# Attention kernel: whole-array products in a row instead of alternating with products on half the columns

## The chip, the cores and the metric

The kernel runs on one core of a Trainium2 chip. The metric is the device time of one execution in microseconds (us), as a median of runs; the profile is one further look at a single execution, with its own span. Engines are named as in the profile: PE is TensorE's matmuls, PEld its weight loads, DVE VectorE, ACT ScalarE, POOL GpSimd, SP the queue that issues most DMAs.

## The reference

A linear attention with a decaying state (2 batch rows, 8 heads, 768 tokens, head width 48) feeds a layer with 4 experts of width 1024, which feeds a two-layer network of width 2048. Only the attention is touched by the change:

```
for t in range(S):
    cur = einsum('bhd,bhe->bhde', u * k[t], v[t])
    y[t] = einsum('bhd,bhde->bhe', r[t], state + cur)
    state = w * state + einsum('bhd,bhe->bhde', k[t], v[t])
x = y, rows of all heads together            # 1536 tokens x 384
x = sum over e of p[:, e] * (relu(x @ w1[e]) @ w2[e])
out = elu(x @ w_in) @ w_out
```

## The kernel before, in words

The attention goes in chunks of 128 tokens, 6 to a batch row, 12 in all (`ci` from 0 to 11; `c` is the chunk's place in its batch row). For a chunk it makes a matrix A of 128 x 128 for each head from scaled r and k (`s2`, L251; then `s2p`, L258, copies it out of the banks under a mask, on DVE, onto a diagonal that POOL has written, L233). It then needs, for a pair of heads, S^T r (the state with the past, L306) plus v^T A (the chunk's own part, L312), summed in one PSUM bank. `s3u` (L272) makes the state's change, and `s3s` (L293, L295, on DVE) the next state S from it.

In `s3` the product with S fills the array: its stationary operand is 112 rows by 112 columns, both heads of a pair at once. The products with A have 48 columns, one head in the lower and one in the upper 64 columns, side by side. For each of the 4 pairs, one product on the whole array is followed by two on halves of the columns. Products are in fp32, and the trace has two records, each with a weight load of its own, for one product. Where `c` is 0 (chunks 0 and 6) there is no past, and the S products fall away. `s3` runs for chunks 2 to 11, so 9 of them have S products: 2, 3, 4, 5, 7, 8, 9, 10, 11.

The first two chunks go another way, before the layers start (`s3f`, L353 and L354): the rows of x are made directly in three groups of 128 (`kk`), each first in products on 64 columns, side by side, then one product on the whole array, which adds the diagonal part `va`. Then `s3x` casts the result (ACT, L468) and makes its low part (DVE, L469), which is the first layer's first operand.

The order is written out by hand. The layers' products (`st1`, L610, and `st2`, L646, on the whole array) go in steps; in the first expert's blocks of 256 tokens one or two attention steps (`a1` with `s2`; `a2`; `a3` with `s3`) are placed behind a step's first product until the attention is over. Every engine runs its instructions in the order of the program, and DVE also splits the weights for the layers (`work`, L505) between the attention's steps. The banks of the attention are three, taken in turn (`bank()`).

```
for p in range(NP):
    if c:
        nc.tensor.matmul(py[0:112, p, :], S of the pair, r of the pair, start=True, stop=False)
    for j in range(2):
        nc.tensor.matmul(py[64 * j:64 * j + m, p, :], v of head 2p + j, A[:, j, p, :], ...)
```

Of the kernel before, what the change touches and what calls it, by code (L numbers as in the profile page):

```python
# [22 lines left out]
P = 128  # L23
B, H, S, D = 2, 8, 768, 48
NP = H // 2          # head pairs; a pair sits on partitions 0-47 and 64-111
NCB = S // P         # 128-token chunks of a batch row
NCH = B * NCB
N = B * S            # tokens
DM = H * D
KD = DM // P  # L30
NE, FF = 4, 1024     # experts, their width
NU = NE + 2          # the second layer's 2048 columns count as two more units
NF = FF // P
NX = 6               # slots for weights in the attention's room
WARM = 12            # products of zeros ahead of the first
NS = (2, 1, 2, 1, 1, 1, 1, 1)    # the attention's steps by step of the layers' first block
BA, BB = 1, 2        # the steps of a block that no weights are split in
TB = 512             # tokens of a block
# [8 lines left out]
# the upper words of float64s, read as float32s: of the largest and the least normal float32  # L47
# [3 lines left out]
class Fast:  # L51
    """Attention in chunks of 128 tokens, decays as w^t and w^-(s+1), which
    needs W_LO <= w <= W_HI (elsewhere w is held there, and the general path is taken).

    Rows of a pair of heads: 64 j + (index in the head). The chunk's part of a head's output,
    with its index on the rows, is v^T A + S^T r, where A[s, t] is (k_s w^-(s+1)).(r_t w^t)
    for s < t and r.u.k for s = t."""
# [27 lines left out]
    def bank(self):  # L85
        """The next bank: of three, and of the two layers' while those wait for the first x."""
        pool, tag = self.banks[self.nbank % len(self.banks)]
        self.nbank += 1
        return pool.tile([P, 512], F32, tag=tag, name=tag)

    def warm(self, n):
        """Products of zeros: the array's clock is halved while it has little to do."""
        nc = self.g.nc
        if self.zero is None:
            self.zero = self.c.tile([P, 512], BF16, name="zero")
            nc.vector.memset(self.zero, 0.0)
        pz = self.g.php.tile([P, 512], F32, tag="ph1", name="ph1")
        for _ in range(n):
            nc.tensor.matmul(pz, self.zero[:, 0:P], self.zero, start=True, stop=True)

    # r, k with their index on the rows
# [9 lines left out]
    # r, k, or v, with the tokens on the rows  # L111
# [49 lines left out]
    def setup_masks(self):  # L161
        nc = self.g.nc
        # 1 where t > s
        mf = self.c.tile([P, P], F32, name="mf")
        nc.gpsimd.memset(mf, 0.0)
        nc.gpsimd.affine_select(
            out=mf, in_=mf, compare_op=ALU.is_ge, fill=1.0, base=0,
            pattern=[[-1, P]], channel_multiplier=1)
        nc.gpsimd.tensor_copy(self.mask, mf)
# [25 lines left out]
    # r or k, scaled  # L195
# [9 lines left out]
    # the keys decayed to the chunk's end  # L205
# [6 lines left out]
    # r.u.k, by entries  # L212
# [8 lines left out]
    # the diagonal  # L221
    def s1d(self, ci):
        nc = self.g.nc
        a0 = self.p2.tile([P, H], F32, tag="a0", name="a0")
        nc.vector.tensor_reduce(out=a0, in_=self.st[ci]["uk"], axis=AX.X, op=ALU.add)  # L225
        if ci < 2:
            # the first chunks' diagonal goes by itself
            self.va[ci] = va = self.p2.tile([P, DM], F32, tag="va", name="va")
            nc.vector.tensor_tensor(
                out=va.rearrange("t (h d) -> t h d", h=H), in0=self.v[ci].rearrange("t (h d) -> t h d", h=H),  # L230
                in1=a0.rearrange("s (h o) -> s h o", o=1).to_broadcast([P, H, D]), op=ALU.mult)
            return
        nc.gpsimd.tensor_tensor(  # L233
            out=self.A[ci % 2].rearrange("s j p t -> s p j t"),
            in0=self.g.ident.rearrange("s (a b t) -> s a b t", a=1, b=1).to_broadcast([P, NP, 2, P]),
            in1=a0.rearrange("s (p j o) -> s p j o", j=2, o=1).to_broadcast([P, NP, 2, P]), op=ALU.mult)
# [6 lines left out]
    def s2(self, ci):  # L243
        nc = self.g.nc
        st = self.st[ci]
        # a bank for each of the two places of a head in its pair
        self.pa[ci] = pa = [self.bank().rearrange("q (p t) -> q p t", p=NP) for j in range(2)]
        for p, j in ([(p, j) for j in range(2) for p in range(NP)] if ci < 2 else
                     [(p, j) for p in range(NP) for j in range(2)]):
            a = 64 * j  # L250
            nc.tensor.matmul(  # L251
                pa[j][:, p, :], st["k"][a:a + D, p, :], st["r"][a:a + D, p, :], start=True, stop=True)
# [7 lines left out]
    # the state's change, and the state  # L260
    def s3u(self, ci):
# [5 lines left out]
        # side by side, a head of a pair in each half of the array's columns  # L267
# [30 lines left out]
    def s3(self, ci):  # L298
# [5 lines left out]
        for p in range(NP):  # L304
            if c:
                nc.tensor.matmul(  # L306
                    py[0:112, p, :], self.S[:, p].rearrange("q j e -> q (j e)")[:, 0:112],
                    st["r"][0:112, p, :], start=True, stop=False)
            for j in range(2):
                # at first, all rows up to the second head's are to be written  # L310
                h, m = 2 * p + j, D if c or j else 64
                nc.tensor.matmul(  # L312
                    py[64 * j:64 * j + m, p, :], v[:, h * D:h * D + m], A[:, j, p, :],
                    start=not c, stop=True)
# [5 lines left out]
        if o:  # L320
            # the rows of all heads together, by way of DRAM
# [8 lines left out]
    # the first chunks': the rows of all heads together at once, v and S between zeros  # L330
# [5 lines left out]
    def s3f(self, ci):  # L336
# [3 lines left out]
        for kk in range(KD):  # L340
            # side by side, 64 rows of x in each half of the array's columns
# [8 lines left out]
            for n in range(max(map(len, ops))):  # L350
                for i, o in enumerate(ops):
                    if n < len(o):
                        nc.tensor.matmul(px[64 * i:64 * (i + 1), kk, :], *o[n], start=not n, stop=False)  # L353
            nc.tensor.matmul(  # L354
                px[:, kk, :], self.va[ci][:, kk * P:(kk + 1) * P], g.ident, start=False, stop=True)
# [8 lines left out]
class General:  # L364
    """Attention for any w: each state entry's recurrence is scanned along the tokens, with
    the key's index on the partitions and one column of the state at a time."""
# [8 lines left out]
    def run(self, ident, xT):  # L375
# [5 lines left out]
        # sel[:, e]: from row e, 64 + e to the rows of their halves; one: from the rows of a  # L381
        # half, with the window that starts at 64 - e, to row e, 64 + e
# [69 lines left out]
class Gen:  # L452
# [40 lines left out]
    def split(self):  # L493
        """The next slice's two parts, in steps; each yields the time it takes of DVE."""
# [15 lines left out]
        # a float64 as two words: a = sign, exponent and the upper 20 fraction bits as a  # L510
        # float32 (0 below its normal range, its largest above), c = the 32 bits below
# [28 lines left out]
    def work(self, budget):  # L540
        """Splits ahead, as far as there are slots, for about so much time of DVE."""
# [25 lines left out]
    def probs(self, dp):  # L567
# [7 lines left out]
        # by expert, then tokens  # L575
# [41 lines left out]
    def evac(self, u, n, ph):  # L617
# [8 lines left out]
        else:  # L626
# [4 lines left out]
            # exp(min(h, 0)) - 1 is 0 where h > 0, and at least h elsewhere  # L631
# [57 lines left out]
    def count(self, c):  # L689
        """How many of w's entries the fast attention holds for."""  # L690
# [13 lines left out]
    def setup(self, ctx):  # L704
# [13 lines left out]
        # slices in the order of their splits: (unit, layer, slice)  # L718
# [3 lines left out]
    def setup2(self, ctx):  # L722
        """What the attention's room is for once it is over."""
# [9 lines left out]
    def layers(self, tb0, before):  # L733
        """Both layers, the first unit in blocks of tb0 tokens. before(u, t0, f) is called
        ahead of a step and gives what is to come after its first product, if anything."""
        pend = []
        for u in range(NU):
            n = TB if u else tb0
            for t0 in range(0, N, n):
                for f in range(NF):  # L740
# [3 lines left out]
                    # the end of a block frees its banks before anything else  # L744
# [15 lines left out]
    def fast(self):  # L760
        tc, nc = self.tc, self.nc
        with ExitStack() as ctx:
# [21 lines left out]
            # attention; the first two chunks before the layers start  # L784
# [30 lines left out]
            self.work(0.1)   # w1, slice 0  # L815
# [7 lines left out]
            self.work(0.1)   # w2, slice 0  # L823
# [24 lines left out]
            for i in range(2, NCH):  # L848
                steps += [(f, c) for f, c in ((a1, i), (a2, i + 1), (a3, i)) if c < NCH]
                if i % 2 == 0 and i > 2:  # L850
                    # two steps after the last a3 of a pair
# [62 lines left out]
def laid_out(r, k, v, w, u, moe_domain_probs, moe_w1, moe_w2, moe2_w_in, moe2_w_out):  # L914
    def heads(a):       # head entries to rows 64 j + d of the pairs, 0 between
# [5 lines left out]
    # by chunk: rows 64 j + d, then r or k, pair, token; and rows of tokens, then r, k, v, entry  # L921
# [11 lines left out]
    # slices of 256 hidden columns: unit, slice, layer, row, then 768 values  # L933
# [31 lines left out]
```

## Time and profile before

| | |
|---|---|
| median of 3 runs | 686.3 us (685.81 to 689.27) |
| span of the profiled execution | 685.3 us; its own time is not listed beside it, the fastest run is 685.81 |
| PE busy | 666.9 us, 3701 records |
| PEld busy | 557.4 us |
| DVE, ACT, POOL busy | 352.6, 211.5, 208.0 us |
| L306, L312 (`s3`) on PE | 16.8 and 17.7 us busy, 72 and 160 records |
| L353, L354 (`s3f`) on PE | 8.3 and 3.9 us busy, 64 and 12 records |

A record's busy time on PE is from its start to its modelled end; records overlap, so what a stretch costs is read from one start to the next. The span is cut into stages by what PE does: the first two chunks (to about 25 us), the attention among the first layer steps (about 25 to 131 us), then the layers alone.

### The profile page before, as it was taken

How to read it: one execution, taken by the hardware profiler on the slowest of the kernel's cores; microseconds unless marked ns; L12 is line 12 of the kernel's file. 1: busy time of each engine (PE TensorE's matmuls, PEld its weight loads, DVE VectorE, ACT ScalarE, POOL GpSimd, SP SyncE). 2: the span in 40 equal slices, each digit the busy share in tenths (PEclk: the TensorE clock that was granted, in tenths of full speed). 3: DMA queues.
4: the chain of work that ended last, by engine and by line, in shares of the span. 5: the costliest groups of instructions: out<-in, count | busy, mean ns of one | idle time of the engine just before them, and what ended most of it. 6: DMA issues, size and time to landing. Idle time of an engine off the chain costs nothing.

```text
span 685.3 us, 9098 instructions
## 1 busy us (share of the span) xinstructions
PE 666.9 (97%) x3701; PEld 557.4 (81%) x3701; DVE 352.6 (51%) x505; ACT 211.5 (31%) x358; POOL 208.0 (30%) x163
## 2 busy tenths in 40 slices
PE   8999999999999999999999999999997999999996
PEld 5788988899888888888888887888875888888884
DVE  7896566324544133422135696569596848212121
ACT  3232221123332113211122123133535454644441
POOL 5564563210002020202021225243744534333331
PEclk7899999999999999999999999999998999999999
DMA  8775542102421003210010221202121100001011
GB/s 256 216 215 165 171 148 69 34 15 70 162 92 47 0 3 107 99 47 0 1 55 38 93 92 47 92 7 88 46 92 46 47 0 1 0 1 47 0 47 52
DMA packets 18661, 48.11 MB, mean 70 GB/s; under 512 B 2145, under 2 KB 7698, under 8 KB 18610
## 3 DMA queue, kind: packets, MB, share of 16 engines
q1 hardware_dynamic: 18464, 47.42, 21.4%
q8 instruction: 31, 0.51, 0.3%
q14 instruction: 20, 0.16, 0.1%
q10 hardware_dynamic: 146, 0.03, 0.0%
HBM read 43.09 MB, written 4.35 MB: 69 GB/s over the span
## 4 chain that ended last, share of the span: by engine, by line
PE 84%; DVE 9%; issue 3%; POOL 2%; ACT 1%; DMA 0%; DVEq 0%; POOLq 0%; ACTq 0%
PE po L646 38%; PE ph L610 37%; PE pa L251 2%; PE pa L306 2%; PE pa L312 2%; DVE raw L519 1%; POOL acc L667 1%; DVE q L530 1%; DVE a L523 1%; DVE g L632 1%; DVE q L520 1%; DVE a L534 1%; DVE hl L623 1%; DVE a L527 1%; POOL wl L535 1%
## 5 line engine op out<-in xcount | busy, mean ns | idle before, releaser
L646 PE MATMUL po<-hh,wh 128*128 128x512 f32 (+1 forms) x504 | 183.4, 364 | 4.9 <-ACT acc L684 4.6
L646 PE MATMUL po<-hl,wh 128*128 128x512 f32 (+1 forms) x504 | 181.9, 361 | 1.9 <-POOL hl L635 1.7
L646 PE MATMUL po<-hh,wl 128*128 128x512 f32 (+1 forms) x504 | 181.5, 360 | 0.0
L610 PE MATMUL ph<-xh,wh 128*128 128x512 f32 (+1 forms) x504 | 177.7, 361 | 0.1
L610 PE MATMUL ph<-xh,wl 128*128 128x512 f32 (+1 forms) x504 | 177.1, 360 | 0.0
L623 DVE SCALAR_TENSOR_TENSOR hl<-ph,hh 128x512 fp32r<-128x512 f32 (+1 forms) x120 | 69.6, 582 | 179.9 <-ACT hh L622 179.2
L622 ACT ACTIVATE hh<-ph 128x512 fp32r<-128x512 f32 (+1 forms) x120 | 61.2, 512 | 281.9 <-PE ph L610 281.9
L610 PE MATMUL ph<-xl,wh 128*128 128x512 f32 (+1 forms) x504 | 126.1, 359 | 0.0
L646 PEld LDWEIGHTS po<-hh,wh 128*128 128x128 f32 x504 | 95.4, 189 | 22.4 <-ACT acc L684 5.0
L646 PEld LDWEIGHTS po<-hl,wh 128*128 128x128 f32 x504 | 95.6, 190 | 17.7 <-POOL hl L635 2.9
L610 PEld LDWEIGHTS ph<-xh,wh 128*128 128x128 f32 x504 | 95.5, 190 | 14.9 <-issue 0.4
L610 PEld LDWEIGHTS ph<-xh,wl 128*128 128x128 f32 x504 | 95.5, 189 | 14.1
L646 PEld LDWEIGHTS po<-hh,wl 128*128 128x128 f32 x504 | 95.5, 190 | 14.0
L610 PEld LDWEIGHTS ph<-xl,wh 128*128 128x128 f32 x504 | 88.3, 189 | 14.1
L635 POOL TENSOR_TENSOR hl<-g,hh 128x512 fp32r<-128x512 f32 x48 | 63.8, 1329 | 100.2 <-ACT hh L634 92.0
L667 POOL TENSOR_TENSOR acc<-acc,t 128x512 f32<-128x512 f32 x27 | 34.1, 1293 | 195.4 <-DVE t L666 195.4
L632 DVE SCALAR_TENSOR_TENSOR g<-m,ph 128x512 f32<-128x512 f32 x48 | 32.9, 684 | 92.0 <-ACT m L630 87.8
L535 POOL TENSOR_TENSOR wl<-a,raw 128x768 fp32r<-128x768 f32 x16 | 29.9, 1868 | 99.2 <-DVE a L534 59.2
L634 ACT CAST hh<-g 128x512 fp32r<-128x512 f32 x48 | 29.8, 622 | 68.0 <-DVE g L632 68.0
L629 ACT ACTIVATE m<-ph 128x512 f32<-128x512 f32 x48 | 28.6, 596 | 28.4 <-PE ph L610 28.2
L505 DVE TENSOR_TENSOR wl<-raw,wh 128x768 fp32r<-128x768 f32 x32 | 33.0, 1032 | 2.3 <-ACT wh L504 1.7
L233 POOL TENSOR_TENSOR A<-ident,a 128x1024 f32<-128x1024 f32 x10 | 20.7, 2071 | 43.5 <-DVE a L225 25.2
(103 smaller groups left out, 513.1 us busy)
## 6 DMA issues: line engine op xcount, KB each, us to landing
raw<-in_ws_dram SPq DMA_DIRECT2D x32, 384.0 KB, 3.0
raw<-in_ws_dram SPq DMA_DIRECT2D x16, 768.0 KB, 4.1
rk<-in_rkv_dram SPq DMA_DIRECT2D x12, 384.0 KB, 5.6
rkT<-in_rkT_dram SPq DMA_DIRECT2D x10, 448.0 KB, 5.2
pb<-pd SPq DMA_DIRECT2D x4, 768.0 KB, 3.9
v<-in_rkv_dram SPq DMA_DIRECT2D x12, 192.0 KB, 6.2
out_dram<-acc SPq DMA_DIRECT2D x9, 256.0 KB, 2.1
xd<-yT SPq DMA_DIRECT2D x10, 192.0 KB, 2.7
```

What stands on the lines that cost most here:

```text
L233: nc.gpsimd.tensor_tensor(out=self.A[ci % 2].rearrange("s j p t -> s p j t"), in0=self.g.ident.rearrange("s (a b t) -> s a b t", a=1, b=1) ...
L505: self.weng.tensor_tensor(out=lo, in0=t, in1=hi.bitcast(F32), op=ALU.subtract)
L535: nc.gpsimd.tensor_tensor(out=lo, in0=af, in1=cf, op=ALU.add)
L610: nc.tensor.matmul(ph[:, 0:n], a[:, kk, c0:c0 + P], b[:, kk], start=q == 0, stop=q == 3 * KD - 1)
L622: nc.scalar.activation(hh[:, 0:n], ph[:, 0:n], AF.Relu)
L623: nc.vector.scalar_tensor_tensor(out=hl[:, 0:n], in0=ph[:, 0:n], scalar=0.0, in1=hh[:, 0:n].bitcast(F32), op0=ALU.max, op1=ALU.subtract)
L629: nc.scalar.activation(m, ph, AF.Relu, scale=-1.0)
L632: nc.vector.scalar_tensor_tensor(out=gg, in0=m, scalar=-1.0, in1=ph, op0=ALU.add, op1=ALU.max)
L634: nc.scalar.copy(hh, gg)
L635: nc.gpsimd.tensor_tensor(out=hl, in0=gg, in1=hh.bitcast(F32), op=ALU.subtract)
L646: nc.tensor.matmul(po[:, 0:n], a[:, ff, i * P:(i + 1) * P], b[:, 0:n], start=f == 0 and q == 0, stop=f == NF - 1 and q == 2)
L667: nc.gpsimd.tensor_tensor(out=a, in0=a, in1=t[:, 0:n], op=ALU.add)
```

## The change

In `s3` the four products with S go first, in a row, then the eight with A. In `s3f` all products on 64 columns of the three groups go first, then the three with `va`. As groups of one bank are now open together, the flag that opens a bank's accumulation is set once, with the first product in that bank, and the later ones only add. Comments and blank lines change too, which moves line numbers (L306 becomes L308, L312 L315, L353 L356, L354 L359, L610 L615, L646 L651).

```
         py = self.bank().rearrange("q (p t) -> q p t", p=NP)
-        for p in range(NP):
-            if c:
+        if c:
+            for p in range(NP):
                 nc.tensor.matmul(
                     py[0:112, p, :], self.S[:, p].rearrange("q j e -> q (j e)")[:, 0:112],
-                    st["r"][0:112, p, :], start=True, stop=False)
+                    st["r"][0:112, p, :], start=not p, stop=False)
+        for p in range(NP):
             for j in range(2):
                 h, m = 2 * p + j, D if c or j else 64
                 nc.tensor.matmul(
                     py[64 * j:64 * j + m, p, :], v[:, h * D:h * D + m], A[:, j, p, :],
-                    start=not c, stop=True)
+                    start=not c, stop=not c or p == NP - 1)
...
             for n in range(max(map(len, ops))):
                 for i, o in enumerate(ops):
                     if n < len(o):
-                        nc.tensor.matmul(px[64 * i:64 * (i + 1), kk, :], *o[n], start=not n, stop=False)
+                        nc.tensor.matmul(
+                            px[64 * i:64 * (i + 1), kk, :], *o[n], start=not n and not kk, stop=False)
+        for kk in range(KD):
             nc.tensor.matmul(
-                px[:, kk, :], self.va[ci][:, kk * P:(kk + 1) * P], g.ident, start=False, stop=True)
+                px[:, kk, :], self.va[ci][:, kk * P:(kk + 1) * P], g.ident, start=False, stop=kk == KD - 1)
```

On PE, at chunk 2's `s3`, between the state's change (L272) and the next layer step; `S_101` is the state, `A_96` the matrix A, `pa_427` the bank; a count is of products.

```order
 L272 MATMUL pa_418<-v,kp_98 48x48 x8
-L306 MATMUL pa_427<-rkT,S_101 112x128
-L312 MATMUL pa_427<-A_96,v 48x128 x2
-L306 MATMUL pa_427<-rkT,S_101 112x128
-L312 MATMUL pa_427<-A_96,v 48x128 x2
...
+L308 MATMUL pa_427<-rkT,S_101 112x128 x4
+L315 MATMUL pa_427<-A_96,v 48x128 x8
```

Before, the pair of rows stands there four times: with the entry from L272, eight changes between halves and whole array. Now there are two. The same products are issued.

On PE, in `s3f` of chunk 0; `va` is the diagonal part, `ph_256` the bank.

```order
 L272 MATMUL po_247<-v,kp_98 48x48 x8
-L353 MATMUL ph_256<-A_96,vp 64x128 x4
-L354 MATMUL ph_256<-ident,va 128x128
-L353 MATMUL ph_256<-A_96,vp 64x128 x4
-L354 MATMUL ph_256<-ident,va 128x128
...
+L356 MATMUL ph_256<-A_96,vp 64x128 x12
+L359 MATMUL ph_256<-ident,va 128x128 x3
```

Before, the pair stands there three times: five changes inside the fifteen products. Now there is one. Chunk 1's `s3f` is moved in the same way. The other engines keep their order.

## Rows read from the trace of the kernel before

**Rows 1.** The page: the chain that ended last, by engine.

```profile
PE 84%; DVE 9%; issue 3%; POOL 2%; ACT 1%; DMA 0%; DVEq 0%; POOLq 0%; ACTq 0%
```

**Rows 2.** Two stretches: length, then busy us of PE, PEld, DVE, ACT, POOL; clock, DMA.

```profile
25.00:57.30 32.30, 30.47 (x290) 25.05 (x291) 31.75 (x48) 10.51 (x20) 22.12 (x15) 1.00 0.74 236
57.30:140.00 82.70, 82.70 (x781) 72.28 (x780) 44.72 (x83) 15.98 (x35) 32.76 (x25) 1.00 0.35 103
```

**Rows 3.** Timeline, PE, chunk 4's s3: start us, length us, instruction, records.

```profile
53.60 0.47 PE L306 MATMUL pa<-rkT,S 112*112 112x128 f32 x2
54.00 0.43 PE L312 MATMUL pa<-A,v 128*48 128x128 f32 x4
54.35 0.47 PE L306 MATMUL pa<-rkT,S 112*112 112x128 f32 x2
...
56.63 0.38 PE L646 MATMUL po<-hh,wh 128*128 128x256 f32 x1
```

**Rows 4.** Timeline, PE: chunk 5's entry from a layer step, and chunk 6.

```profile
64.49 0.38 PE L306 MATMUL pa<-rkT,S 112*112 112x128 f32 x2
64.80 0.43 PE L312 MATMUL pa<-A,v 128*48 128x128 f32 x4
...
75.77 1.05 PE L312 MATMUL pa<-A,v 128*64 128x128 f32 x16
76.75 0.39 PE L646 MATMUL po<-hh,wh 128*128 128x256 f32 x1
```

**Rows 5.** L306: records' ns min/median/max, and its idle time (us, times).

```profile
L306 PEld LDWEIGHTS pa<-rkT,S x72: 172/176/178, 30.5 to 130.6; 112*112 112x112 f32 x72
L306 PE MATMUL pa<-rkT,S x72: 270/273/364, 30.5 to 130.7; 112*112 112x128 f32 x72
...
  issue: 5.0, 27
```

**Rows 6.** Timeline, weight loads of chunk 4's first product.

```profile
53.59 0.27 PEld L306 LDWEIGHTS pa<-rkT,S 112*112 112x112 f32 x2
```

**Rows 7.** The chain of waits, first two chunks: start us, length us, what.

```profile
15.87 1.05 PE ph L353 x8
16.92 0.73 PE ph L354 x2
...
21.83 0.81 PE pa L353 x12
22.64 0.42 PE pa L354 x2
...
24.53 0.49 ACT xh L468
```

**Rows 8.** Timeline, DVE, about the first layer step; idle before and its releaser.

```profile
23.73 0.55 DVE L225 TENSOR_REDUCE a<-uk 128x8 f32<-128x384 f32 x1 [0.89 <-POOL uk L218]
25.04 0.56 DVE L469 TENSOR_TENSOR xl<-pa,xh 128x384 fp32r<-128x384 f32 x1 [0.76 <-ACT xh L468]
```

**Rows 9.** Timeline, PE and DVE: where PE waited for DVE.

```profile
30.45 0.47 PE L306 MATMUL pa<-rkT,S 112*112 112x128 f32 x2 [1.20 <-DVE A L258]
...
36.00 1.13 PE L251 MATMUL pa<-rkT 48*128 48x128 f32 x14 [0.57 <-DVE Z L293]
...
48.81 0.94 DVE L505 TENSOR_TENSOR wl<-raw,wh 128x768 fp32r<-128x768 f32 x1
...
49.82 0.37 PE L610 MATMUL ph<-xh,wl 128*128 128x256 f32 x1
```

**Rows 10.** Timeline: chunk 7's state, and the next product that takes its bank.

```profile
87.42 0.36 DVE L293 TENSOR_TENSOR Z<-pa,S 48x192 f32<-48x192 f32 x1
...
91.65 1.16 PE L251 MATMUL pa<-rkT 48*128 48x128 f32 x16
```

**Rows 11.** Stretches about the early clock (columns as in rows 2).

```profile
5.50:7.35 1.85, 0.00 (x0) 0.00 (x1) 1.28 (x4) 0.14 (x1) 1.64 (x3) 1.00 0.88 246
7.50:21.00 13.50, 13.50 (x96) 11.11 (x96) 11.40 (x22) 2.82 (x5) 4.76 (x5) 0.50 1.04 296
```

## The prediction, made before the run

> **What bounds the kernel now.** I read the chain of waits first: PE holds 84% of it [rows 1], so a microsecond that PE saves counts where PE is what the others wait for. The busy times by stretch then show that this isn't so everywhere [rows 2]. From 25.0 to 57.3 us DVE is busy for 31.75 of 32.30 us: it has no room either, and PE waits for it three times in its first 25 us. From 57.3 to 140 us DVE is busy for 44.72 of 82.70 us and PE for all of it. So the attention has an opening (to 25 us), a part where DVE and PE press on each other (to about 50 us), and a part that is PE's alone. In the timeline I then look at what a change between whole-array and half-column products costs: not at the lengths of records, which overlap, but from one start to the next.
>
> **What the change gives at one `s3`.** In chunk 4 a pair's whole-array product starts at 53.60, its halves at 54.00, the next whole-array product at 54.35 [rows 3]. So a pair takes 0.40 + 0.35 = 0.76 us, and the chunk 56.63 - 53.60 = 3.03 us.
>
> What would these products take in a row? *Whole array:* where chunk 5 comes from a layer step, already on the whole array, two records start 0.38 - 0.27 = 0.11 us apart (length of both, less one record's median 0.273) [rows 4, 5]; behind a switch it is 0.47 - 0.27 = 0.20 [rows 3]. So a record's pace is 0.11, a product's 0.22, and 0.40 holds a switch of 0.18. *Halves:* chunk 6 has no state products, and its 16 records stand in a row: 76.75 - 75.77 = 0.98 us with the switch behind them [rows 4].
>
> The row of the changed chunk: first record to second 0.20, six further records at 0.11 = 0.66, the last to the first half 0.20, then 0.98: together 2.04 us. The gain is 3.03 - 2.04 = **0.99 us for each chunk** with state products. The same gap stands on the weight loads, which sat idle 27 times before L306, 5.0 us in all [rows 5]: three times in each of nine chunks, all gone with the change; what is left of the gain is the way from whole array to halves. The rows are given to 0.01 us, so the pace may be 0.10 to 0.12: six records move the gain by 0.06 either way. Counted the other way, as three pairs less what two whole-array and four half records (0.98 / 4 = 0.24) take, the lowest is 3 x (0.76 - 0.24 - 0.24) = 0.84. Bounds: 0.84 and 1.05.
>
> The edits of the flags cost nothing: the same records are issued, no other engine's order changes, and no DMA is moved. The row makes S needed at once for all pairs, as before for the first, and makes A needed about 1.06 us later, which can only help. The copy to yT (ACT) still waits for the last product. No wait is added.
>
> **Where that gain counts.** *Chunks 2 and 3: nothing.* PE waits at 30.45 for DVE's copy of A (1.20 us) and at 36.00 for Z to leave a bank (0.57), and at 49.82 a layer product is stretched to 0.37 because DVE's split of the weights ends at 48.81 + 0.94 = 49.75 [rows 9]. DVE has no idle time ahead of that [rows 2], so whatever PE saves in chunks 2 and 3 (2 x 0.99, and 0.2 at chunk 2, whose halves waited for A) becomes longer waits at 36.00 and 49.82. *Chunks 4, 5, 7, 8, 9, 10, 11: all of it*, 7 x 0.99 = 6.9 us. Their s3 starts after 53.6, and from 57.3 DVE is idle nearly half the time. What would be late next is the bank that Z frees for the following `s2`: chunk 7 shows it, read out by 87.42 + 0.36 = 87.78, taken at 91.65 [rows 10], 3.9 us of lead, of which the change takes at most 1.0 since both follow the same `s3`.
>
> **The opening.** In `s3f` of chunk 0 a group's halves and whole-array product take 1.05 + 0.73 = 1.78 us at a granted clock of 0.50, that is 1.2 GHz [rows 7, 11]. At twice the records' pace above (0.11 for a half record with two side by side, 0.22 for a whole-array one) eight and two of them need 0.88 + 0.44 = 1.32. A pair of switches costs some 0.46 there, and two pairs go: 0.9 us. In `s3f` of chunk 1, with the clock up to 1.00 (2.4 GHz) by then, 12 half records take 0.81 (12 x 0.055 = 0.66) and a product 0.42 (0.22 without a switch) [rows 7]: 0.35 for a pair, two pairs 0.7. So the cast of x (ACT) could start some 1.6 us earlier than at 24.53 [rows 7]. But its reader, DVE at 25.04, waited for it only 0.76 us; before that DVE ended L225 at 23.73 + 0.55 = 24.28, and that one had waited for POOL, which the change doesn't touch [rows 8]. DVE, then without rest to 57.3, starts **0.75 us** earlier and passes just that on to 49.82. Bounds: 1.6 if POOL and DVE move up too; -0.5 if the clock, at 0.50 up to 21.0 and at 1.00 in the stretch from 25 [rows 2, 11], rises some 3 us later, so that the second `s3f` stays at half pace.
>
> **The sum.** 6.9 + 0.75 = 7.7 us off the profiled execution's 685.3, giving 677.6. The median of the runs stands 1.0 us over that span, so I forecast 686.3 - 7.7 = **678.6 us**. After 140 us PE still leads the chain, and what follows is released by PE's own progress, so it should only move up.
>
> **The rivals.**
> - *All of it counts.* If DVE's work in 25 to 50 us shortens as well (its L505 and L295 vary with what POOL does), chunks 2 and 3 add 2.2 and the opening up to 0.8: 675.6 us. Against it: DVE's 98% in that stretch [rows 2].
> - *A second gate.* Some wait after 57.3 takes half of the seven chunks' gain: 686.3 - 0.75 - 3.5 = 682.0. Against it: the lead of rows 10. For it: shorter steps leave less time to DMAs, which I haven't all followed.
> - *The change doesn't do what it says.* If the 0.20 between records belonged to each new product and not to the switch, the row would cost what the pairs do: 686.3. Against it: 0.11 at chunk 5's entry [rows 4].
> - *Weight loads in a row don't overlap.* In the trace the two loads of one whole-array product take 0.27 us together, at 0.176 each, so the second starts 0.10 after the first, while the first record, up to 0.364 long, still runs [rows 3, 5, 6]. If they did not overlap, eight records would take 8 x (0.176 + 0.11) = 2.29, the chunk 3.27 instead of 3.03, nine chunks 2.2 more: 688.5. The Trainium skill ("TensorE: Matmul & The Clock Gate", part 3, "What overlaps and what doesn't") says that a weight load overlaps a running matmul only where their row groups differ, which would speak against rows of products on all rows. By that rule 688.5; by the rows, where loads of the same rows do overlap, the sum above.
> - *Slower: the clock falls in the longer waits.* PE's waits between 25 and 50 us grow from 1.9 us in all to about 4, the longest (at 36.00) to about 1.75. Early in the trace PE had no record for 1.85 us, and the clock was 0.50 from 7.5 to 21 us [rows 11]. If it falls at 35 us in the same way, PE does half its work for as long as that lasts, while DVE still covers some 4 us. The point from which it decides: 2 x (7.7 + 4) = 23 us at 1.2 GHz eat the gain; 33 us of it cost 5 more: 691. Against it: the fall came when only sparse products had run; after the 1.20 us at 30.45 the clock stayed 1.00 [rows 2, 9].
>
> **How the numbers follow.** Forecast 0.76, all of it 0.08, second gate 0.08, no effect 0.03, no overlap 0.02, slower by the clock 0.03. The forecast's own bounds are 7 x 0.84 - 0.5 = 5.4 and 7 x 1.05 + 1.6 = 9.0: 680.9 to 677.3; with a scatter of runs of up to 1 us and most of the first two rivals the range is 675.6 to 682.5. A measurement tells some 0.5%, 3.4 us, from no change: the line lies at 682.9, so the second gate stands just on the fast side of it and I split it. Faster 0.76 + 0.08 + 0.04 = 0.88; same 0.04 + 0.03 + 0.02 = 0.09; slower 0.03.
>
> **What would show it.** Right: each later `s3` with states takes about 2.0 us from its first record to the next layer step; whole-array records 0.11 apart; the 27 idle stretches gone; the waits at 36 and 50 us still there, the first grown to about 1.7 us, with DVE full until about 56. Wrong: whole-array records 0.2 or more apart in the row; new PE waits after 57 us; a granted clock under 1.00 between 25 and 140 us; DVE with gaps before 50 us and PE ahead of it.

## The result, and the profile after

The changed kernel takes **679.6 us** (median of 4 runs, 678.58 to 682.09) against 687.2 for the kernel before beside it (4 runs, 685.81 to 689.27): ratio 0.9887, interval 0.9864 to 0.9911, which is some 7.8 us by the ratio (the medians differ by 7.6). The profiled execution has a span of 677.1 us against 685.3, 8.2 less; its own time is 678.96 us.

The chain of waits of the changed kernel, by engine, answers to [rows 1]:

```profile
PE 81%; DVE 9%; issue 3%; DMA 2%; POOL 2%; ACT 1%; SPq 0%; DVEq 0%; POOLq 0%; ACTq 0%
```

The same stretches as in [rows 2], with the same columns, and one piece of the first:

```profile
25.00:57.30 32.30, 31.21 (x296) 28.20 (x294) 31.19 (x46) 9.80 (x18) 20.20 (x15) 0.84 0.74 235
57.30:140.00 82.70, 82.70 (x829) 78.10 (x829) 47.45 (x89) 17.45 (x38) 34.86 (x26) 1.00 0.36 102
...
26.00:36.00 10.00, 8.91 (x60) 7.68 (x59) 9.79 (x16) 1.71 (x4) 7.00 (x5) 0.50 0.73 234
```

Two things stand here. From 57.3 us on, PE is still busy throughout, and in the same 82.7 us it now has 829 records instead of 781: nothing new waits there. And from 26 to 36 us the granted clock is 0.50, where it was 1.00 before. That is the sign that the prediction's last rival was to show.

The timeline of PE about `s3` of chunks 4 and 5 (start, length, instruction, records), against [rows 3, 4]:

```profile
52.36 0.56 PE L272 MATMUL pa<-v,kp 128*48 128x48 f32 x16
52.86 1.13 PE L308 MATMUL pa<-rkT,S 112*112 112x128 f32 x8
53.91 1.08 PE L315 MATMUL pa<-A,v 128*48 128x128 f32 x16
54.93 0.39 PE L651 MATMUL po<-hh,wh 128*128 128x256 f32 x1
...
62.79 1.04 PE L308 MATMUL pa<-rkT,S 112*112 112x128 f32 x8
63.76 1.08 PE L315 MATMUL pa<-A,v 128*48 128x128 f32 x16
64.77 0.39 PE L651 MATMUL po<-hh,wh 128*128 128x256 f32 x1
```

Chunk 4 takes 54.93 - 52.86 = 2.07 us instead of 3.03. Its eight whole-array records take 53.91 - 52.86 = 1.05, 0.13 each with the switches at both ends. The view of L308 by source, against [rows 5] (ns min/median/max of its weight loads, then what ended its idle time, us and times):

```profile
L308 PEld LDWEIGHTS pa<-rkT,S x72: 173/177/310, 29.8 to 122.5; 112*112 112x112 f32 x72
...
  DVE A L258: 2.3, 2
```

The 27 idle stretches of 5.0 us on the weight loads are gone; what is left is the wait for A.

**Where the 8.2 us came from.** I cut the span at two places that every kernel here has: L225, DVE's sum for chunk 2 (the last of DVE's work that hangs on POOL's products for that chunk, [rows 8]), and the state's change on PE ahead of chunk 4's `s3` (L272, 53.10 us before). A third cut is the layer step behind chunk 11's `s3`.

| us | before | changed | less |
|---|---|---|---|
| L225 starts | 23.73 | 23.09 | 0.64 |
| from there to L272 of chunk 4 | 29.37 | 29.27 | 0.10 |
| from there to the step behind chunk 11 | 78.19 | 71.47 | 6.72 |
| from there to the end of the span | 554.01 | 553.27 | 0.74 |

So 6.72 us, 0.96 for each of seven chunks, came from chunks 4 to 11, and the stretch with chunks 2 and 3 gave 0.10. The last row is scatter: over all the runs of this study it lies between 552.99 and 554.43, in no order that follows an edit.

### The profile page after: what moved, and what is told of

It is laid out like the page before. It is cut to its first block, busy times and chain, and to the rows that moved or that the text cites. A ratio compares the mean times of both kernels' runs of the same rounds, so it can differ in the third digit from the quotient of the medians.

```text
span 677.1 us, 9098 instructions
## 1 busy us (share of the span) xinstructions
PE 657.4 (97%) x3701; PEld 557.4 (82%) x3701; DVE 352.9 (52%) x505; ACT 211.4 (31%) x358; POOL 206.6 (31%) x163
## 4 chain that ended last, share of the span: by engine, by line
PE 81%; DVE 9%; issue 3%; DMA 2%; POOL 2%; ACT 1%; SPq 0%; DVEq 0%; POOLq 0%; ACTq 0%
PE po L651 39%; PE ph L615 38%; PE pa L315 2%; PE pa L308 1%; PE pa L251 1%; DMA rk<-in_rkv_dram 1%; DVE raw L524 1%; POOL acc L672 1%; DMA ub<-in_u_dram 1%; DVE q L535 1%; DVE a L528 1%; DVE g L637 1%; DVE q L525 1%; DVE a L539 1%; DVE a L532 1%
## 5 line engine op out<-in xcount | busy, mean ns | idle before, releaser
L651 PE MATMUL po<-hh,wh 128*128 128x512 f32 (+1 forms) x504 | 183.2, 363 | 4.9 <-ACT acc L689 4.6
L651 PE MATMUL po<-hl,wh 128*128 128x512 f32 (+1 forms) x504 | 181.8, 361 | 1.9 <-POOL hl L640 1.7
L651 PE MATMUL po<-hh,wl 128*128 128x512 f32 (+1 forms) x504 | 181.4, 360 | 0.0
L615 PE MATMUL ph<-xh,wh 128*128 128x512 f32 (+1 forms) x504 | 178.4, 362 | 0.1
L615 PE MATMUL ph<-xh,wl 128*128 128x512 f32 (+1 forms) x504 | 177.8, 361 | 0.0
L615 PE MATMUL ph<-xl,wh 128*128 128x512 f32 (+1 forms) x504 | 126.9, 360 | 2.1 <-DVE xl L474 2.1
L651 PEld LDWEIGHTS po<-hh,wh 128*128 128x128 f32 x504 | 95.2, 189 | 22.5 <-ACT acc L689 5.0
L651 PEld LDWEIGHTS po<-hl,wh 128*128 128x128 f32 x504 | 95.4, 189 | 17.7 <-POOL hl L640 3.1
L615 PEld LDWEIGHTS ph<-xh,wh 128*128 128x128 f32 x504 | 96.1, 191 | 15.1 <-issue 0.5
L615 PEld LDWEIGHTS ph<-xh,wl 128*128 128x128 f32 x504 | 96.0, 191 | 14.2
L651 PEld LDWEIGHTS po<-hh,wl 128*128 128x128 f32 x504 | 95.4, 189 | 13.9
L615 PEld LDWEIGHTS ph<-xl,wh 128*128 128x128 f32 x504 | 88.9, 191 | 16.4 <-DVE xl L474 2.3
```

The source lines that it names most:

```text
L615: nc.tensor.matmul(ph[:, 0:n], a[:, kk, c0:c0 + P], b[:, kk], start=q == 0, stop=q == 3 * KD - 1)
L651: nc.tensor.matmul(po[:, 0:n], a[:, ff, i * P:(i + 1) * P], b[:, 0:n], start=f == 0 and q == 0, stop=f == NF - 1 and q == 2)
```

## The experiments

All diffs are against the changed kernel, unless said. This table has every profiled execution's cuts, as above; "clock" is where the granted clock was 0.50 between 22 and 50 us. Ratios are to the kernel before on the same chip; its medians there were 687.19 us beside the changed kernel, 688.06 beside e1 to e4, 688.63 beside e5 to e8 and 686.78 beside e9 to e12, so medians of different groups are compared by their ratios.

| kernel | median us, ratio [interval] | L225 | to chunk 4 | chunks 4 to 11 | clock 0.50 |
|---|---|---|---|---|---|
| before | | 23.73 | 29.37 | 78.19 | none |
| changed | 679.6, 0.9887 [0.9864, 0.9911] | 23.09 | 29.27 | 71.47 | 26 to 36 |
| e1_s3_only | 679.55, 0.9872 [0.9851, 0.9892] | 23.80 | 31.22 | 71.46 | 36 to 42 |
| e2_s3f_only | 686.27, 0.9985 [0.9969, 1.0001] | 23.36 | 29.28 | 78.19 | 26 to 29 |
| e3_from_chunk4 | 680.91, 0.9908 [0.9875, 0.9941] | 24.19 | 29.30 | 71.46 | 27 to 30 |
| e4_halves_first | 677.68, 0.9851 [0.9828, 0.9873] | 23.38 | 28.94 | 69.83 | 31 to 34 |
| e5_rows_of_two | one run, 682.66 | 23.79 | 30.17 | 73.70 | 26 to 29, 36 to 40 |
| e6_warm_gap | 680.61, 0.9869 [0.9833, 0.9905] | 23.48 | 31.29 | 71.46 | 36 to 42 |
| e7_pool_split | 680.92, 0.9883 [0.9845, 0.9921] | 23.66 | 29.84 | 71.47 | 26 to 29, 36 to 39 |
| e8_pool_split_old | 688.35, 0.9991 [0.9972, 1.001] | 23.59 | 31.03 | 78.19 | 31 to 37 |
| e9_warm3 | 680.05, 0.9893 [0.9869, 0.9917] | 23.83 | 28.95 | 71.46 | none |
| e10_warm3_pool | 679.51, 0.9887 [0.9864, 0.991] | 23.00 | 28.99 | 71.46 | none |
| e11_warm3_halves | 677.73, 0.9862 [0.9836, 0.9887] | 23.69 | 29.36 | 69.83 | none |
| e12_warm3_pool_halves | 678.57, 0.9876 [0.9853, 0.99] | 24.36 | 28.99 | 69.83 | none |

### e1_s3_only and e2_s3f_only: the two parts of the change alone

In e1 the opening (`s3f`) alternates as before, in e2 `s3` does:

```
e1, in s3f:
...
-        for kk in range(KD):
...
             nc.tensor.matmul(
-                px[:, kk, :], self.va[ci][:, kk * P:(kk + 1) * P], g.ident, start=False, stop=kk == KD - 1)
+                px[:, kk, :], self.va[ci][:, kk * P:(kk + 1) * P], g.ident, start=False, stop=True)
e2, in s3:
-        if c:
-            for p in range(NP):
+        for p in range(NP):
+            if c:
...
```

> Only the chunks' s3 has its products in rows; the first two chunks alternate as before. Theory (seven chunks give 0.96 to 0.99 us each, the opening gives about 0.75): 6.8 us under the kernel before (ratio 0.990); layer product at the weights' gate (49.82 us before) at the same place within 0.2 us, then each s3 2.05 us long. Rival (all nine chunks count): 8.8 us under (0.987), the gate near 47.8. Rival (the opening gives most of what was measured): under 4 us (above 0.994).

> Only the first two chunks have rows; s3 alternates as before. Theory: 0.75 us under the kernel before (ratio 0.999, not to be told from 1), the gate at about 49.05 us instead of 49.82, each s3 3.03 us long. Rival (PE's whole saving in the opening counts): 1.6 to 2.5 us under, the gate at 48.2 or earlier. Rival (the clock falls in the longer wait and costs time): at or above the kernel before.

Measured: e1 is as fast as the whole change (0.9872 against 0.9887, the intervals overlap); e2's ratio of 0.9985 is worth 1.0 us, and its interval reaches 1. The table shows why: the 6.7 us are in e1's chunks 4 to 11 and in none of e2's. e2's first cut, 23.36, is 0.2 us ahead of the earliest with the old opening (23.59 to 23.80), but the others with the new opening lie on both sides of those (23.00 to 24.36). The opening isn't shown to give anything by this cut; a finer one stands in the part on the prediction.

e1 has a surprise: from L225 to chunk 4 it takes 31.22 us, 1.9 more than the kernel before. A stretch of its windows, and DVE's timeline (idle time before an instruction and its releaser in brackets):

```profile
36.00:42.00 6.00, 5.93 (x32) 5.69 (x32) 5.94 (x9) 0.00 (x0) 3.49 (x4) 0.50 0.84 261
```

```profile
46.39 1.48 DVE L508 TENSOR_TENSOR wl<-raw,wh 128x768 fp32r<-128x768 f32 x1 [1.30 <-ACT wh L507]
```

The clock is 0.50 for 6 us. DVE doesn't cover all of it: it goes idle for 1.30 us, since the high part that it subtracts came late from ACT. I come back to this at e6.

### e3_from_chunk4: no gain from chunks 2 and 3?

```
+        if ci < 4:
+            for p in range(NP):
+                if c:
...
+        else:
```

(The old alternating loop stands under the `if`, the rows of the change under the `else`.)

> As the changed kernel, but chunks 2 and 3 alternate in s3 as before. Theory (what PE saves there only becomes a wait for DVE): the same time as the changed kernel within 0.3 us, if the clock stays at 1.00; PE's waits between 25 and 50 us shrink by about 2 us. Rival (all chunks count): 2 us above the changed kernel. If the clock falls at 26 us as it did there, PE has lost its slack and the gate moves: up to 2 us above.

Measured: 29.30 us from L225 to chunk 4, against 29.27 with the rows in all chunks, and 71.46 behind it. PE's waits in the trace, from 22 to 140 us (who waits, for whom, us, times, longest):

```profile
PE ph L627 <- DVE xl L486: 2.1, 1, 2.1
PE pa L309 <- DVE A L258: 0.9, 1, 0.9
PE pa L251 <- DVE Z L293: 0.6, 1, 0.6
```

The wait of 0.6 for Z is that of [rows 9], again with alternating products ahead of it. So the order in chunks 2 and 3 is worth nothing that shows. The clock fell in this execution too, for 3 us; among those where it held, the kernel before takes 29.37 with alternating products and e9 to e12 take 28.95 to 29.36 with rows, so in these executions no more than 0.4 of the some 2 us that PE saves there came through. That DVE sets the pace is read from its busy time, 28.18 of those 29.37 us in the kernel before and 28.68 of 29.27 in the changed one; no run shows it by making DVE's work shorter (e7 and e10 try). The median, 680.91, can't be told from that of the changed kernel (ratios 0.9908 and 0.9887, the intervals overlap).

### e4_halves_first and e5_rows_of_two: is it the number of switches?

e4 puts the A products first and the S products behind them; the state's change, also on halves, comes just ahead. A change of mode, or switch, is a step between products on the whole array and products on halves of its columns: e4 leaves one of them in such a chunk instead of three. Its lower A products have 64 columns instead of 48, as chunk 6's have [rows 4], so that the A products write every row of the bank that S's products add to. e5 puts two pairs in a row at a time, one pair of switches more than the change.

```
e4:
+        for p in range(NP):
+            for j in range(2):
+                h, m = 2 * p + j, D if j else 64
+                nc.tensor.matmul(
+                    py[64 * j:64 * j + m, p, :], v[:, h * D:h * D + m], A[:, j, p, :],
+                    start=not c or not p, stop=not c)
         if c:
             for p in range(NP):
                 nc.tensor.matmul(
...
-                    st["r"][0:112, p, :], start=not p, stop=False)
-        for p in range(NP):
...
+                    st["r"][0:112, p, :], start=False, stop=p == NP - 1)
e5:
...
+        for q in (0, 2):
+            if c:
+                for p in (q, q + 1):
...
+            for p in (q, q + 1):
+                for j in range(2):
...
```

> As the changed kernel, but in s3 the products on halves stand in front of those on the whole array, so that a chunk which comes from the state's change (halves) and goes on to a layer step (whole array) has one switch instead of three. Theory (a pair of switches costs 0.18 + 0.14 = 0.32 us): s3 takes 1.75 us instead of 2.07 in chunks 4, 7, 8, 9 and 10, the same in 5 and 11, where the row comes from a layer step: 5 x 0.32 = 1.6 us under the changed kernel. Rival (what a chunk gained was the loads' overlap inside rows, not the switches): no difference.

> As the changed kernel, but s3 goes in two rows: two products on the whole array, their four on halves, then again. Theory (a pair of switches costs 0.32 us wherever it stands): a chunk's s3 takes 2.07 + 0.32 = 2.4 us from its first record to the next layer step; from chunk 4's state change to the layer step behind chunk 11 it is 71.5 + 7 x 0.32 = 73.7 us. Rival (a row helps only once it is long, or most of the gain comes from the first pair's order): 2.07 or near 3.0 us.

Measured: PE's timeline at chunk 4, first of e4:

```profile
52.32 0.56 PE L272 MATMUL pa<-v,kp 128*48 128x48 f32 x16
52.72 1.05 PE L309 MATMUL pa<-A,v 128*64 128x128 f32 x16
53.70 1.13 PE L314 MATMUL pa<-rkT,S 112*112 112x128 f32 x8
54.58 0.36 PE L650 MATMUL po<-hh,wh 128*128 128x256 f32 x1
```

and then of e5:

```profile
54.45 0.69 PE L309 MATMUL pa<-rkT,S 112*112 112x128 f32 x4
55.07 0.65 PE L315 MATMUL pa<-A,v 128*48 128x128 f32 x8
55.65 0.69 PE L309 MATMUL pa<-rkT,S 112*112 112x128 f32 x4
56.27 0.65 PE L315 MATMUL pa<-A,v 128*48 128x128 f32 x8
56.84 0.39 PE L651 MATMUL po<-hh,wh 128*128 128x256 f32 x1
```

e5's chunk 4 takes 56.84 - 54.45 = 2.39 us, 0.32 more than the changed kernel's 2.07, and its chunks 4 to 11 take 73.70 instead of 71.47: 7 x 0.32. e4 gains 1.64 us there (69.83), 0.33 for each of the five chunks whose `s3` stands behind a state's change (chunks 5 and 11 come from a layer step, as [rows 4] show for chunk 5, and have as many switches either way). Counted from its first record, e4's `s3` takes 1.86 us and not the expected 1.75; 0.10 more is saved ahead of it, since its first product follows the state's change (L272) after 0.40 instead of 0.50 us. Three pairs of switches at 0.32 are also the change's own 0.96. The 64 columns of e4's lower products aren't what saves: where its halves come behind a layer step (chunk 5), they take 1.01 us to the next row, as the 48-column ones of the changed kernel's chunk 4 do (1.02). The same products, in three more orders, cost what their switches cost: this is shown. Of all kernels e4 has the lowest median and ratio, 677.68 and 0.9851.

### e6_warm_gap: does the clock fall because of PE's wait at the first layer step?

Eight products of zeros, which nothing reads, are put ahead of the layers, where the changed kernel's PE waits for xl:

```
+            at.warm(8)
             self.layers(256, before)
```

> As the changed kernel, with 8 products of zeros on the otherwise idle array ahead of the first layer step (they compute nothing that is used). Theory: the clock stays at 1.00 past 26 us, where it fell in the changed kernel; since DVE sets the end of that stretch, chunk 4 still comes 29.3 us behind DVE's last sum for chunk 2 (L225), and the median stays within 1 us of the changed kernel's. Rival (the fallen clock costs time in that stretch): chunk 4 comes 1 us or more sooner behind L225, and the median falls by as much.

Measured: no gain, 680.61 us. Two stretches of its windows:

```profile
26.00:34.00 8.00, 5.17 (x61) 4.27 (x58) 7.86 (x14) 2.02 (x4) 5.30 (x5) 1.00 0.73 250
36.00:42.00 6.00, 6.00 (x36) 5.55 (x38) 5.94 (x9) 0.03 (x1) 3.31 (x4) 0.50 0.91 246
```

The fall at 26 us is gone, but the clock falls at 36, as in e1. A PE that isn't slowed waits for A instead, 2.2 us, and again for the weights' split and for Z, 0.7 and 0.8. And this fall costs more: 31.29 us to chunk 4, later than either forecast and against the changed kernel's 29.27. With one wait filled the clock still fell, only later.

### e7_pool_split and e8_pool_split_old: is DVE the gate?

If DVE sets the pace to chunk 4, it should help to take work from it. Two of its splits of the weights go to POOL, in e7 in the changed kernel, in e8 with the old order of both parts:

```
-            self.weng.tensor_tensor(out=lo, in0=t, in1=hi.bitcast(F32), op=ALU.subtract)
+            eng = nc.gpsimd if self.nspl in (4, 6) else self.weng
+            eng.tensor_tensor(out=lo, in0=t, in1=hi.bitcast(F32), op=ALU.subtract)
```

> As the changed kernel, but POOL instead of DVE makes the low parts of two weight slices (the fourth and the sixth), which frees DVE for 0.95 and 1.65 us between 35 and 47 us. Theory (DVE is the gate that swallows what PE saves in chunks 2 and 3): chunk 4's state change comes 1.0 to 2.5 us sooner behind DVE's L225 than 29.3, and the median is 1 to 2 us under the changed kernel. Rival (the gate is something else, a DMA or PE itself): 29.3 us again.

> The same relief of DVE, on the kernel with the old order of products in both places. Theory: PE, with s3 3.03 us long in chunks 2 and 3, is then the bound itself, so the relief brings less: chunk 4's state change at 28.0 to 28.8 us behind L225, against 27 to 28 with rows; so with DVE relieved the rows gain up to 1 us more than without. Rival (chunks 2 and 3 give nothing in any case): the same distance from L225 with the old order as with rows.

Measured: no gain in either (29.84 and 31.03 us to chunk 4). Since the clock fell in both, for different times, the two can't be compared with each other; e10 has the same relief with the clock up.

### e9 to e12: the clock held, then the rest one by one

e9 fills three waits with zeros that nothing reads: at the first layer step, at chunk 2's `s3` and ahead of chunk 3's `s2`. e10 is e9 with e7's edit, e11 is e9 with e4's, e12 has all three.

```
+            at.warm(8)
             self.layers(256, before)
...
         pu = self.s3u(ci)
+        if ci == 2:
+            self.warm(8, "po0")
...
             def a1(c):
+                if c == 3:
+                    at.warm(5, "po0")
```

> As the changed kernel, with products of zeros (8, 8 and 5, used by nothing) in all three waits that the change leaves between 22 and 36 us: ahead of the first layer step, of chunk 2's s3 and of chunk 3's s2. Theory (a fallen clock is what takes the stretch beyond DVE's 29.3 us): the clock stays at 1.00 from 22 to 50 us, chunk 4's state change comes 29.3 us behind DVE's L225, and the median is 0 to 1.5 us under the changed kernel's. Rival (the waits do no harm): nothing changes but the clock; median the same, 31 us behind L225 is still seen. Rival (the zeros stand in the way): 30 us or more at a clock of 1.00.

> The same with the two weight slices split on POOL instead of DVE. Theory (with the clock up, DVE alone is the gate, and what it is relieved of comes through): 27.0 to 28.5 us behind L225, 1 to 2 us under the run with the zeros alone. Rival (POOL's own work becomes the gate): 29.3 or more.

> The zeros with s3's halves ahead of its whole-array products. Theory: chunk 4 comes 29.0 to 29.3 us behind L225; from there to the end of the attention as with halves first, 1.6 us under rows alone; median 1.6 us under the run with the zeros alone, near 677.

> Zeros, POOL's two slices and halves first together. Theory: the parts add, 3 us under the run with the zeros alone: 675.5 to 677. Rival (POOL's two slices push its kp and uk, so that A comes late for s3, the more so as halves first needs it sooner): no better than zeros with halves first.

Measured: the clock is 1.00 from 22 to 50 us in all four. e9's windows:

```profile
22.00:36.00 14.00, 12.22 (x103) 8.45 (x103) 11.94 (x19) 4.38 (x8) 10.48 (x8) 1.00 0.68 215
36.00:50.00 14.00, 13.80 (x140) 12.71 (x141) 13.79 (x21) 3.96 (x8) 9.44 (x7) 1.00 0.76 206
```

From L225 to chunk 4 they take 28.95, 28.99, 29.36 and 28.99 us: what the changed kernel (29.27) and the kernel before (29.37) take too, within 0.5. So in the changed kernel's own profile 10 us at half the clock cost some 0.3 us at most, and the ratios agree: 0.9893 for e9, 0.9887 without the zeros. e10 shows what became of the work taken from DVE; its timeline of DVE and POOL about 37 us:

```profile
35.57 1.95 POOL L513 TENSOR_TENSOR wl<-raw,wh 128x768 fp32r<-128x768 f32 x1
37.49 1.01 POOL L216 TENSOR_TENSOR uk<-rk,ub 128x384 f32<-128x384 f32 x1
38.58 1.33 POOL L218 TENSOR_TENSOR uk<-uk,rk 128x384 f32<-128x384 f32 x1
```

```profile
37.60 1.46 DVE L199 TENSOR_TENSOR rkT<-rkT,T 112x512 f32<-112x512 f32 x1
38.98 1.48 DVE L199 TENSOR_TENSOR rkT<-rkT,Kd 112x512 f32<-112x512 f32 x1
```

The split takes POOL 1.95 us and pushes POOL's own products to where DVE does L199, which then takes 1.46 and 1.48 us; in e9 the same two take 0.90 and 0.68, and in the changed kernel's opening, with POOL idle beside it, L199 takes 0.67 and 0.68. DVE gives back what it was spared: from L225 to chunk 4 it is busy for 28.53 of 28.99 us, in e9 for 28.51 of 28.95. So e10 shows why the relief brought nothing; whether PE would gain from a DVE that is really relieved, it doesn't show. Of the three edits only the order of e4 adds something, in chunks 4 to 11: 69.83 with the zeros or without. e12 isn't faster than e11 (0.9876 and 0.9862), as its rival had it. e11 and e4 can't be told apart (0.9862 and 0.9851), so the zeros can be left out. **e4 is the version to take**; that it beats the changed kernel rests on the 1.64 us in its rows, since the intervals of the two ratios overlap.

## Why the prediction was right, point by point

- *The time.* 678.6 was forecast, 679.6 measured; 7.7 us off the span, 8.2 measured. Of the 8.2, the 6.72 of chunks 4 to 11 are the forecast's mechanism; that the rest (0.74 of scatter, 0.64 at L225, 0.10) comes near the forecast's 0.75 for the opening is luck, as shown below.
- *The gain at one `s3`.* 0.99 was forecast, 0.96 measured, since the row takes 2.07 instead of 2.04. What the row was built from, the pace of 0.11 and the switches at each end, held (1.05 us from the first whole-array record to the first half, 1.06 forecast). The 0.03 too much is in the halves: 1.02 us, where the 0.98 was taken from chunk 6, whose halves come behind other halves and not behind a switch; e4 and e5 show the price of a pair of switches, 0.32 to 0.33, in two further orders.
- *Which chunks count.* Seven, as forecast: 6.72 against 6.9, by the 0.03 at each chunk. e3 shows nothing to be had from chunks 2 and 3.
- *The opening, 0.75: right in size by luck, wrong in its reason.* The gate at 49.82 did move to 49.06, by 0.76, as PE's timeline of the changed kernel has it:

```profile
49.06 0.38 PE L615 MATMUL ph<-xh,wl 128*128 128x256 f32 x1
```

  But the step said that DVE regains its wait of 0.76 ahead of xl [rows 8] and passes it on. It regained it and lost it again two instructions later. DVE in the changed kernel:

```profile
23.09 0.55 DVE L225 TENSOR_REDUCE a<-uk 128x8 f32<-128x384 f32 x1 [1.98 <-POOL uk L218]
23.56 0.55 DVE L474 TENSOR_TENSOR xl<-pa,xh 128x384 fp32r<-128x384 f32 x1
24.02 0.34 DVE L293 TENSOR_TENSOR Z<-pa,Sp 48x192 f32<-48x192 f32 x1
24.39 1.50 DVE L295 TENSOR_TENSOR S<-Z,T 48x192 f32<-48x192 f32 x1
```

and POOL beside it:

```profile
20.94 1.05 POOL L216 TENSOR_TENSOR uk<-rk,ub 128x384 f32<-128x384 f32 x1 [6.24 <-DMA rk<-in_rkv_dram]
22.06 0.99 POOL L218 TENSOR_TENSOR uk<-uk,rk 128x384 f32<-128x384 f32 x1
23.78 1.90 POOL L233 TENSOR_TENSOR A<-ident,a 128x1024 f32<-128x1024 f32 x1 [0.73 <-DVE a L225]
```

The same two engines in the kernel before, POOL and then DVE:

```profile
20.50 1.52 POOL L216 TENSOR_TENSOR uk<-rk,ub 128x384 f32<-128x384 f32 x1 [5.37 <-DMA rk<-in_rkv_dram]
22.10 1.59 POOL L218 TENSOR_TENSOR uk<-uk,rk 128x384 f32<-128x384 f32 x1
24.42 1.90 POOL L233 TENSOR_TENSOR A<-ident,a 128x1024 f32<-128x1024 f32 x1 [0.73 <-DVE a L225]
```

```profile
25.89 0.64 DVE L295 TENSOR_TENSOR S<-Z,T 48x192 f32<-48x192 f32 x1
```

  S (L295) starts 1.50 us earlier, and takes 1.50 us instead of 0.64. In both kernels it ends 0.21 us behind POOL's A (24.39 + 1.50 = 25.89 against 23.78 + 1.90 = 25.68; 26.53 against 26.32; in e9 and e10 L295 ends 0.20 to 0.21 behind the A of a later chunk), and A starts 0.69 behind L225. So from L225 on nothing was won (0.10), and what moved the gate is L225 itself, by 0.64. It follows POOL's two products, which took 2.04 us instead of 3.11, started later by 0.44, when their DMA landed. Two thirds of the 0.64 were there before any product that the change moves could matter. DVE's same sum for chunk 1, in the kernel before and then in the changed one:

```profile
17.54 0.55 DVE L225 TENSOR_REDUCE a<-uk 128x8 f32<-128x384 f32 x1
```

```profile
17.11 0.55 DVE L225 TENSOR_REDUCE a<-uk 128x8 f32<-128x384 f32 x1
```

  0.43 of the 0.64 stands here already, and in both traces DVE has waited for nothing since a DMA that held it until 10.08 and 9.90 us. From this sum to the one for chunk 2 it is 6.19 us before and 5.98 in the changed kernel; the other two with the old opening take 6.19 (e1) and 6.03 (e8), the other ten with the new one 5.96 to 6.30. So some 0.2 us at most of what moved L225 can be the change's, and that isn't clear of the spread between executions. The step that failed is the one that booked DVE's regained wait of 0.76 as a gain; it cost little, since the term was a tenth of the sum.
- *The second gate, all of it, no effect:* none happened. 82.70 of 82.70 us busy on PE from 57.3 on, e3's 29.30, and 2.07 us at chunk 4 speak against each.
- *Weight loads in a row don't overlap.* Eight whole-array records took 1.05 us, with a load of 0.177 (median) for each: the loads do run beside products on the same rows. The rule of the Trainium skill ("TensorE: Matmul & The Clock Gate", part 3, "What overlaps and what doesn't"), by which the change would have been slower, does not hold in this trace. Another of its rules fits: the Trainium skill's "TensorEngine Tiling (Array Packing)", "Key Properties", says that a change of mode drains the array. That changes cost time is what this trace shows, 0.32 us for a pair; that a drain is what takes it, no row here shows.
- *The clock falls.* I gave that 0.03 as a way to a slower kernel. It did fall, in the changed kernel's profile and in all of e1 to e8, and it did not make the kernel slower. The wait ahead of it, 2.11 us for xl at the first layer step, stands in none of the forecast's waits. A fall isn't free everywhere: in e1, e6 and e8, where the clock was 0.50 for some 6 us from 31 or 36 us on, chunk 4 came 31.03 to 31.29 us behind L225, some 2 us more than with the clock up, still far less than the gain. The step had taken the cover into account (DVE's 4 us) and asked for 23 us at 1.2 GHz; 10 came, and then PE had no wait left at 36 us: it used up its waits instead of adding time. So the sign named for a wrong prediction, a clock under 1.00 between 25 and 140 us, was too strict, and the wait at 36 us, which should have grown to 1.7, can't be seen for the same reason. In e1, where the clock held until 36, PE waited 2.18 at A, 0.66 at the split and 0.81 at Z, 3.65 us in all, near the forecast of about 4; but the longest was the one at A, and not, as forecast, that for Z at 36 us.

## What to carry to other kernels

Read what a change of mode costs from one start to the next on PE, count the changes that an order makes, and put products of one mode next to each other, with what comes ahead and behind counted in; here a pair of changes was 0.32 us, and the same products in four orders took what their count said. Multiply only over the places where PE is what others wait for. And before a regained wait is booked as a gain on an engine, look at the two or three instructions behind it: one that runs beside another engine's long instruction may stretch to that one's end, as L295 beside POOL's A did here (1.50 us instead of 0.64).

## What the runs showed of the hardware that was not expected

The clock fell to 0.50 in the midst of dense work, after waits of about 2 us on PE. The changed kernel's PE waits, from 22 us on:

```profile
PE ph L615 <- DVE xl L474: 2.1, 1, 2.1
PE pa L308 <- DVE A L258: 1.1, 1, 1.1
```

The first ends at 24.16 us and the clock is 0.50 from about 26. In e1 a wait of 2.18 us ends at 30.53, shorter ones follow, and it is 0.50 from 36. All nine traces with a fall between 22 and 50 us (the changed kernel, e1 to e8) have a wait of 2.1 us or more ahead of it. In the kernel before the longest wait was 1.20 [rows 9] and it held; with the waits filled (e9 to e12, none over 0.94) it held as well. How the fall hangs on the lengths of the waits is not settled by these runs, and each kernel was profiled in one execution only.

In the opening, too, the clock's way differs from one profiled execution to the next: 0.50 until about 21 us in the kernel before, until about 16 in the changed one, and in e4 1.00 until 17 and then 0.50 to nearly 21. The first layer product moves with it (25.06, 21.08 and 22.91 us), while L225 (23.73, 23.09, 23.38) moves by 0.64 at most.
